# Second-level products placed differently in two PSUM tiles, and result stores issued from ScalarE's queue

## Chip, cores and metric

The kernel runs on one core of a Trainium2 chip. The metric is device time in microseconds (us) of one execution; the time before is the median of three runs. Engines are named as in the profile: PE is TensorE (PEld its weight loads), DVE is VectorE, ACT is ScalarE, POOL is GpSimd, SP is SyncE, which here only issues DMAs. A "q" behind an engine's name is its sequencer, which issues DMAs.

## What is computed

An attention block is followed by a feed-forward block. In the attention block (4 batches, 8 heads, 768 positions, 64 columns a head) queries and keys are assigned to 16 centroids, and a query attends only to keys of its own cluster. The result, 3072 x 512, is the input x of the second block, which the change concerns:

```python
def _moe_ref(x, w_in, w_out):
    h = x @ w_in            # (3072, 512) @ (512, 2048)
    r = np.maximum(h, 0.0)
    g = r * r
    return (g @ w_out).astype(np.float32)   # (3072, 2048) @ (2048, 512)
```

All is float32.

## The kernel before

The attention of all 16 pairs of heads comes first (to about 320 us), in an order written out by hand. Then the four batches go through the feed-forward block one after the other, in the order `FEED` = (1, 2, 3, 0). For each batch `up` makes g = relu(x w_in) squared, held transposed with the hidden dimension on the partitions, and a `down` function multiplies g by `w_out`.

Both products use a Strassen-like scheme: a matrix product is cut into 2 x 2 blocks, and seven block products of sums of blocks take the place of eight. The first batch uses `down` (L804), with one level of this scheme. It also prepares, in `make_right`, sums of the right-hand blocks for a second level and stores them in DRAM (`w_far`). During this first `down`, the hand-written order ends (`manual.close()`, L833); what comes after is put in order by the program that lays out the queues, by priorities and its own estimates, so the order on an engine can differ from that of the source.

The other three batches use `down_2` (L993). It treats 384 rows in two parts: a third of each half with one level (`product`, L1001, matmuls recorded at L1004) and two thirds with two levels (`second_level`, L903). `down_2` first issues three first-level products (1, 2, 4), then the whole second level, then calls `behind_pair`, which loads the next batch's x (`load_x`, L1108), then makes first-level products 7, 5, 6 and 3 and stores its own results (`osb`, L1039).

`second_level` goes through the seven outer products in the order `ORDER` = (5, 1, 7, 6, 2, 3, 4). Each is a group of seven inner products of 128 x 128 blocks with a contraction of 512, made by `times` (L894) as four float32 matmuls, which the trace records as eight matmuls and eight weight loads. In the text P1 to P7 are the seven in source order (L955 to L963). Within a group:

- `bank_tile` gives two PSUM tiles, `one` and `two`, each 128 x 512 float32, out of six such buffers. `spot(bank, i)` is the i-th block of 128 columns.
- P1 goes to block 0 of `one`, and ScalarE copies it out at once (`copied`, L956).
- P2, P3 and P5 go to `one` as well; P4, P6 and P7 go to `two`.
- P3, P4, P5 and P7 read their right operand from four slots (`slot(1)`, `slot(2)`, `slot(0)`, `slot(3)`) in SBUF. Each slot has one buffer; `load_right` (L879) issues the DMAs that refill them for the next group, four of 256 KB, on SP's queue.
- VectorE subtracts in place for P6's left operand (L958), between P2 and P6, prepares the left sums of the next group (`parts`, L930) and then adds the products up: four sums (L970 to L981) read PSUM, and `outer` (L914) adds their result r into c11, c12, c21, c22. After group 5, one more subtraction (L984) restores s2's sum for later groups.

At the end four DMAs of 256 KB (L986) store c22, c11, c12 and c21 in the output, on SP's queue. Of these tiles, c22 is complete after outer product 6, c11 after 2, c12 after 3 and c21 after 4.

When the next batch's x has come, `up` forms sums of it on VectorE (`x_sums`, L540, recorded at L538) and starts its matmuls (L767).

Of the kernel before, what the change touches and what calls it, by code (L numbers as in the profile page):

```python
# [18 lines left out]
P = 128  # L19
# [6 lines left out]
def kernel(  # L26
# [10 lines left out]
    nc = tc.nc  # L37
# [499 lines left out]
    def sub(out, a, b, eng=nc.vector):  # L537
        return eng.tensor_tensor(out=out, in0=a, in1=b, op=ALU.subtract)  # L538
# [161 lines left out]
    def bank_tile(width):  # L700
        return banks.tile([P, width], F32, name="bank", tag="bank")
# [142 lines left out]
    def right(j):  # L844
        return {1: w_q[0][0], 2: w_q[1][0], 3: w_q[1][1], 4: w_t[4], 5: w_t[1], 6: w_t[2],
                7: w_t[3]}[j]
# [11 lines left out]
    def s_home(i):  # L858
        return home[2 * i][:, 0 : F2 * PAIR].rearrange("p (f n) -> p f n", f=F2)

    def slot(k):
        first = F2 * PAIR + (k % 2) * F4 * P
        return home[k // 2 * 2][:, first : first + F4 * P].rearrange("p (f n) -> p f n", f=F4)

    def quarters(y):
        return [[y[:, F4 * g : F4 * (g + 1), P * m : P * (m + 1)] for m in range(2)] for g in range(2)]
# [12 lines left out]
    def load_right(j, *which):  # L879
        for k in which:  # L880
            nc.sync.dma_start(slot(k), w_far[j - 1, k].rearrange("p (f n) -> p f n", f=F4))

    def blocks(g, cols):
        return [[g[:, F2 * g2 : F2 * (g2 + 1), h, cols] for g2 in range(2)] for h in range(2)]
# [9 lines left out]
    def times(bank, left, rhs):  # L894
        for f in range(F4):
            nc.tensor.matmul(  # L896
                bank, lhsT=left[:, f], rhs=rhs[:, f], start=(f == 0), stop=(f == F4 - 1)
            )

    def plus(out, one, two):  # L900
        nc.vector.tensor_tensor(out=out, in0=one, in1=two, op=ALU.add)

    def second_level(b, g, sums_behind):  # L903
        a = blocks(g, slice(0, PAIR))
        s1, s2 = (s_home(i) for i in range(2))
        left = {1: a[0][0], 2: a[0][1], 3: s1, 4: a[1][1], 5: s1, 6: s2, 7: a[1][0]}
        work = xp.tile([P, KT * S], F32, name="work", tag="x1")
        c11, c12, c21 = (
            tp.tile([P, 4 * P], F32, name=f"c{to}", tag=f"x_t{t}")
            for to, t in ((11, 1), (12, 2), (21, 4))  # L910
        )
        c22 = spare.tile([P, 4 * P], F32, name="c22")

        def outer(j, r):  # L914
            if j == 1:
                plus(c12, c11, c22)
            elif j == 7:
                plus(c21, c11, r)
            elif j == 6:
                plus(c12, c12, r)  # L920
                plus(c21, c21, r)
                plus(c22, c22, c21)
            elif j == 2:
                plus(c11, c11, r)
            elif j == 3:
                plus(c12, c12, r)
            elif j == 4:
                sub(c21, c21, r)

        def parts(n):  # L930
            j = ORDER[n]
            x = [[left[j][:, F4 * g2 : F4 * (g2 + 1), P * i : P * (i + 1)] for g2 in range(2)]
                 for i in range(2)]
            s = sp.tile([P, 2, F4, P], F32, name="l2", tag=f"s{n % 2 + 1}")
            plus(s[:, 0], x[1][0], x[1][1])
            sub(s[:, 1], s[:, 0], x[0][0])
            sub(x[1][0], x[0][0], x[1][0])
            return x, s

        ahead = parts(0)  # L940
        yield
        for n, j in enumerate(ORDER):
            x, s = ahead
            y = quarters(right(j))
            first = 5 * P * (n % 2)
            copied = work[:, first : first + P]
            r = {5: c22, 1: c11}.get(j)
            if r is None:
                r = work[:, first + P : first + 5 * P]
            one, two = bank_tile(4 * P), bank_tile(4 * P)  # L950

            def spot(bank, i, n=1):
                return bank[:, P * i : P * (i + n)]

            times(spot(one, 0), x[0][0], y[0][0])  # L955
            nc.scalar.copy(out=copied, in_=spot(one, 0))  # L956
            times(spot(one, 1), x[0][1], y[1][0])
            sub(x[0][1], x[0][1], s[:, 1])  # L958
            times(spot(one, 2), s[:, 1], slot(1))
            times(spot(two, 0), x[1][0], slot(2))  # L960
            times(spot(one, 3), s[:, 0], slot(0))
            times(spot(two, 1), x[0][1], y[1][1])
            times(spot(two, 2), x[1][1], slot(3))  # L963
            if n + 1 < len(ORDER):
                ahead = parts(n + 1)
                load_right(ORDER[n + 1], 1, 2, 0, 3)
            else:
                sums_behind()

            plus(  # L970
                spot(r, 0, 2).rearrange("p (m n) -> p m n", m=2),
                spot(one, 1, 2).rearrange("p (m n) -> p m n", m=2),
                copied.unsqueeze(1).to_broadcast([P, 2, P]),
            )
            plus(spot(r, 2), spot(two, 0), spot(r, 1))
            plus(
                r.rearrange("p (i m n) -> p i m n", i=2, m=2)[:, :, 1],
                spot(one, 3).unsqueeze(1).to_broadcast([P, 2, P]),
                spot(r, 1, 2).rearrange("p (i n) -> p i n", i=2),
            )  # L980
            plus(spot(r, 1, 2), spot(two, 1, 2), spot(r, 1, 2))  # L981
            outer(j, r)
            if j == 5:
                sub(s1, a[0][1], s2)  # L984
        for to, (h, m) in ((c22, (1, 1)), (c11, (0, 0)), (c12, (0, 1)), (c21, (1, 0))):
            nc.sync.dma_start(  # L986
                out_view[b, NB * h : NB * h + 2, :, M2 * m : M2 * (m + 1)].rearrange(
                    "j p m -> p j m"
                ),
                to.rearrange("p (i m) -> p i m", i=2),  # L990
            )

    def down_2(b, g, behind_pair):  # L993
# [20 lines left out]
        def sums():  # L1014
# [3 lines left out]
            sub(a[1][0], a[0][0], a[1][0])  # L1018

        pair = second_level(b, g, sums)  # L1020
        next(pair)
        next(pair, None)
# [290 lines left out]
```

## Time and profile before

| | |
|---|---|
| time, median of 3 runs | 903.16 us (900.92 to 904.25) |
| time of the profiled execution | 900.14 us |
| span of the profiled execution, first to last instruction | 898.0 us |
| granted TensorE clock | 1.000 |
| second-level matmuls (L896) | x1176, first at 550.3, last at 878.4 us |
| copy of P1 (L956) | x21, 266 ns each |
| loads home<-w_far | x84, 256.0 KB each |
| stores out_dram<-c (L986) | x12, 256.0 KB each |

Lines of the profile name first the source line, the engine, the operation and its output and input, with buffer numbers left out: `bank` is a PSUM tile of `bank_tile`, `home` holds the slots and two of the left operands, `l` a pair of left sums, `g` the activations, `w_out` and `w_t` right operands, `work` the copy and r, `c` a result tile. In a timeline, a line begins with the start and the length of a run of like instructions in us. Weight loads overlap with matmuls. [...]

### The profile page before, as it was taken

The numbers are of one execution on the slowest core, as the hardware profiler recorded it, in microseconds if no ns is written. First come the engines' busy times: TensorE is split into PE (matmuls) and PEld (weight loads), VectorE is DVE, ScalarE is ACT, GpSimd is POOL, SyncE is SP. The second block draws the span as 40 slices with busy tenths as digits, with TensorE's granted clock in tenths as the row PEclk, the third lists the DMA queues.
The fourth block names the chain that finished last, engine by engine and source line by source line (L and its number), as shares of the span: only waits on it lengthen the run. The fifth ranks groups of instructions, "written<-read, shape, count | busy, mean of one in ns | idle before, by whom it ended". The sixth has DMA issues, their size and how long they took to land.

```text
span 898.0 us, 13177 instructions
## 1 busy us (share of the span) xinstructions
PE 889.4 (99%) x5043; PEld 583.8 (65%) x5043; DVE 680.9 (76%) x1107; ACT 321.3 (36%) x479; POOL 156.9 (17%) x168
## 2 busy tenths in 40 slices
PE   9999999999999999999999999999999999999997
PEld 5444444444444455578885559996557997556996
DVE  6798888888888999999525757757675785577683
ACT  5876677776676657630001110001111000111000
POOL 0000100000100257710022510013420004250000
PEclk9999999999999999999999999999999999999999
DMA  7767878677663246215400001560000563000351
GB/s 247 180 190 214 226 224 199 178 210 207 196 155 93 84 164 201 74 48 216 159 24 0 1 0 48 184 215 24 0 1 1 170 194 106 1 0 1 123 183 51
DMA packets 116442, 107.63 MB, mean 120 GB/s; under 512 B 56491, under 2 KB 93971, under 8 KB 115859
## 3 DMA queue, kind: packets, MB, share of 16 engines
q1 hardware_dynamic: 108130, 96.45, 36.0%
q10 hardware_dynamic: 8240, 10.26, 3.6%
q8 instruction: 42, 0.69, 0.3%
q14 instruction: 30, 0.24, 0.1%
HBM read 67.42 MB, written 28.25 MB: 107 GB/s over the span
## 4 chain that ended last, share of the span: by engine, by line
PE 91%; DVE 5%; DMA 1%; issue 1%; ACT 1%; DVEq 0%
PE bank L767 28%; PE bank L896 14%; PE sc L441 13%; PE av_a L475 9%; PE bank L821 8%; PE bank L1004 8%; PE av_b L475 4%; PE sc L450 3%; PE sc L329 1%; PE sc L494 1%; DVE g L724 1%; DVE w_raw L149 1%; DMA home<-w_far 1%; DVE w_raw L145 1%; DVE total L460 1%
## 5 line engine op out<-in xcount | busy, mean ns | idle before, releaser
L457 ACT ACTIVATE ex<-sc 128x1024 f32<-128x1024 f32 x144 | 144.4, 1026 | 38.0 <-PE sc L441 33.0
L724 DVE TENSOR_TENSOR g<-bank,g 128x384 f32<-128x384 f32 x192 | 102.6, 553 | 71.0 <-PE bank L767 67.9
L441 PE MATMUL sc<-qkT 64*128 64x512 f32 (+1 forms) x768 | 150.6, 484 | 0.0
L767 PE MATMUL bank<-xT,w_s 128*128 128x384 f32 x256 | 93.2, 487 | 0.9 <-DVE g L724 0.9
L767 PE MATMUL bank<-xT,w_in 128*128 128x384 f32 x256 | 93.2, 487 | 0.0
L441 PEld LDWEIGHTS sc<-qkT 64*128 64x128 f32 x768 | 65.9, 188 | 41.9 <-issue 30.1
L767 PE MATMUL bank<-x_t,w_s 128*128 128x384 f32 x256 | 93.0, 486 | 0.0
L475 PE MATMUL av_a<-ex,v_raw 128*64 128x512 f32 x384 | 85.9, 596 | 0.0
L558 POOL TENSOR_TENSOR w_s<-w_in 128x256 f32<-128x256 f32 x32 | 25.7, 804 | 337.4 <-PE bank L1004 155.7
L460 DVE TENSOR_TENSOR total<-total,ex 128x1024 f32<-128x1024 f32 x64 | 78.7, 1229 | 6.5
L161 POOL TENSOR_TENSOR w_in<-w_in,w_raw 128x512 int32<-128x512 int32 x16 | 22.1, 1379 | 295.2 <-DVE w_in L153 295.2
L730 ACT COPY g<-bank 128x384 f32<-128x384 f32 x32 | 15.3, 479 | 160.5 <-PE bank L767 160.5
L767 PEld LDWEIGHTS bank<-xT,w_s 128*128 128x128 f32 x256 | 48.5, 190 | 35.5 <-issue 2.1
L767 PEld LDWEIGHTS bank<-x_t,w_s 128*128 128x128 f32 x256 | 48.6, 190 | 33.9
L767 PEld LDWEIGHTS bank<-xT,w_in 128*128 128x128 f32 x256 | 48.5, 190 | 33.8 <-DVE g L538 0.6
L475 PEld LDWEIGHTS av_a<-ex,v_raw 128*64 128x64 f32 x384 | 26.1, 137 | 51.0 <-issue 50.7
L450 PE MATMUL sc<-rows 64*128 64x512 bf16 (+1 forms) x360 | 59.0, 323 | 0.3 <-DVE sums_t L503 0.3
L745 ACT ACTIVATE g<-g 128x384 f32<-128x384 f32 x53 | 27.4, 517 | 74.3 <-DVE g L724 74.3
L767 PE MATMUL bank<-x_t,w_in 128*128 128x384 f32 x128 | 46.5, 486 | 0.0
L956 ACT COPY work<-bank 128x128 f32<-128x128 f32 x21 | 5.6, 266 | 112.7 <-PE bank L896 112.7
L748 DVE SCALAR_TENSOR_TENSOR g<-g 128x384 f32<-128x384 f32 x75 | 43.5, 582 | 1.6
L896 PE MATMUL bank<-home,l 128*128 128x128 f32 x336 | 44.4, 275 | 0.0
(183 smaller groups left out, 1459.2 us busy)
## 6 DMA issues: line engine op xcount, KB each, us to landing
home<-w_far SPq DMA_DIRECT2D x84, 256.0 KB
words<-flat SPq DMA_DIRECT2D x26, 384.0 KB
w_raw<-in_moe_w_in_dram SPq DMA_DIRECT2D x16, 512.0 KB
w_raw<-in_moe_w_out_dram SPq DMA_DIRECT2D x16, 512.0 KB
w_far<-home SPq DMA_DIRECT2D x28, 256.0 KB
v_raw<-in_v_dram SPq DMA_DIRECT2D x16, 384.0 KB
rb<-far_r SPq DMA_DIRECT2D x32, 192.0 KB
q_raw<-in_q_dram ACTq DMA_DIRECT2D x12, 384.0 KB
```

The source lines that it names most:

```text
L441: nc.tensor.matmul(sc[i][:, e, cols], lhsT=qkT[pair][rows, NCH + c], rhs=qkT[pair][rows, n.start // P : n.stop // P], start=first, stop=no ...
L450: nc.tensor.matmul(sc[i][:, e, cols], lhsT=ohT[pair][rows, 1, c * P : (c + 1) * P], rhs=ohT[pair][rows, 0, columns(i)], start=first, stop= ...
L457: nc.scalar.activation(out=ex[i], in_=sc.pop(i), func=ACT.Exp, scale=SCALE)
L460: eng.tensor_tensor(out=out, in0=a, in1=b, op=ALU.add)
L475: nc.tensor.matmul(bank[D * e : D * (e + 1), 0 : n.stop - n.start], lhsT=raw_v[pair][:, e, c], rhs=ex[i][:, e, cols], start=c == 0, stop=c ...
L724: nc.vector.tensor_tensor(out=out, in0=bank, in1=to, op=ALU.add)
L745: nc.scalar.activation(out=to, in_=to, func=ACT.Relu)
L748: nc.vector.scalar_tensor_tensor(out=to, in0=to, scalar=0.0, in1=to, op0=ALU.max, op1=ALU.mult)
L767: nc.tensor.matmul(bank, lhsT=operands[j][0][:, kk], rhs=operands[j][1][:, kk], start=(kk == 0), stop=(kk == H2 - 1),)
L821: nc.tensor.matmul(bank, lhsT=left[:, f], rhs=right[:, f], start=(f == 0), stop=(f == F2 - 1))
L896: nc.tensor.matmul(bank, lhsT=left[:, f], rhs=rhs[:, f], start=(f == 0), stop=(f == F4 - 1))
L1004: nc.tensor.matmul(bank, lhsT=left[:, f], rhs=right(j)[:, f], start=(f == 0), stop=(f == F2 - 1))
```

## The change

The seven products keep their order in the source and their operands. P1 stays in block 0 of `one`. P2, P3, P4 and P5 go to blocks 0 to 3 of `two`, and P6 and P7 to blocks 1 and 2 of `one`. The four sums that read PSUM follow their products to the new places. The four stores of `second_level` are issued from ScalarE's queue instead of SP's.

```diff
             times(spot(one, 0), x[0][0], y[0][0])
             nc.scalar.copy(out=copied, in_=spot(one, 0))
-            times(spot(one, 1), x[0][1], y[1][0])
+            times(spot(two, 0), x[0][1], y[1][0])
             sub(x[0][1], x[0][1], s[:, 1])
-            times(spot(one, 2), s[:, 1], slot(1))
-            times(spot(two, 0), x[1][0], slot(2))
-            times(spot(one, 3), s[:, 0], slot(0))
-            times(spot(two, 1), x[0][1], y[1][1])
-            times(spot(two, 2), x[1][1], slot(3))
+            times(spot(two, 1), s[:, 1], slot(1))
+            times(spot(two, 2), x[1][0], slot(2))
+            times(spot(two, 3), s[:, 0], slot(0))
+            times(spot(one, 1), x[0][1], y[1][1])
+            times(spot(one, 2), x[1][1], slot(3))
...
             plus(
                 spot(r, 0, 2).rearrange("p (m n) -> p m n", m=2),
-                spot(one, 1, 2).rearrange("p (m n) -> p m n", m=2),
+                spot(two, 0, 2).rearrange("p (m n) -> p m n", m=2),
                 copied.unsqueeze(1).to_broadcast([P, 2, P]),
             )
-            plus(spot(r, 2), spot(two, 0), spot(r, 1))
+            plus(spot(r, 2), spot(two, 2), spot(r, 1))
             plus(
                 r.rearrange("p (i m n) -> p i m n", i=2, m=2)[:, :, 1],
-                spot(one, 3).unsqueeze(1).to_broadcast([P, 2, P]),
+                spot(two, 3).unsqueeze(1).to_broadcast([P, 2, P]),
                 spot(r, 1, 2).rearrange("p (i n) -> p i n", i=2),
             )
-            plus(spot(r, 1, 2), spot(two, 1, 2), spot(r, 1, 2))
+            plus(spot(r, 1, 2), spot(one, 1, 2), spot(r, 1, 2))
             outer(j, r)
...
         for to, (h, m) in ((c22, (1, 1)), (c11, (0, 0)), (c12, (0, 1)), (c21, (1, 0))):
-            nc.sync.dma_start(
+            nc.scalar.dma_start(
                 out_view[b, NB * h : NB * h + 2, :, M2 * m : M2 * (m + 1)].rearrange(
```

## The prediction

> **What bounds the kernel now.** I read the page's table of engines first, then the chain that ended last, then the timeline of one second-level group, then the waits.
>
> ```profile
> PE 889.4 (99%) x5043; PEld 583.8 (65%) x5043; DVE 680.9 (76%) x1107; ACT 321.3 (36%) x479; POOL 156.9 (17%) x168
> PE 91%; DVE 5%; DMA 1%; issue 1%; ACT 1%; DVEq 0%
> ```
>
> TensorE is occupied 99% of the span and is 91% of the chain, so only time taken out of TensorE's own stream shortens the kernel. The change touches one stage, the second-level products (L955 to L963, all recorded at L896), which run three times, for the batches after the first. The view of three stretches, each from the first second-level matmul to the start of the next L1004 product, gives their length:
>
> ```profile
> 550.31:595.52 45.21, 45.05 (x394) 44.29 (x392) 33.21 (x58) 2.24 (x8) 0.00 (x0) 1.00 0.54 163
> 691.93:737.15 45.22, 45.05 (x393) 44.34 (x392) 33.28 (x58) 2.23 (x8) 0.00 (x0) 1.00 0.53 164
> 833.57:878.56 44.99, 44.99 (x394) 44.37 (x392) 33.22 (x58) 2.24 (x8) 0.00 (x0) 1.00 0.50 159
> ```
>
> Columns: length, then busy time of TensorE, its weight loads, VectorE, ScalarE and GpSimd, clock, DMA share and GB/s. TensorE looks full (45.05 of 45.21), but a matmul's end is modelled, so the busy sum hides short gaps; starts must be compared. The timeline of one group (seven products P1 to P7 in source order, eight instructions each) shows them:
>
> ```profile
> 563.16 1.06 PE L896 MATMUL bank<-w_t,g 128*128 128x128 f32 x8
> ...
> 564.05 0.61 PE L896 MATMUL bank<-home,g 128*128 128x128 f32 x4
> 564.25 0.27 ACT L956 COPY work<-bank 128x128 f32<-128x128 f32 x1 [6.16 <-PE bank L896]
> 564.57 0.97 PEld L896 LDWEIGHTS bank<-w_t,g 128*128 128x128 f32 x8
> 564.57 1.16 PE L896 MATMUL bank<-w_t,g 128*128 128x128 f32 x8
> ...
> 565.57 1.06 PE L896 MATMUL bank<-home,l 128*128 128x128 f32 x8
> ...
> 566.46 0.61 PE L896 MATMUL bank<-home,g 128*128 128x128 f32 x4
> ...
> 566.91 1.06 PE L896 MATMUL bank<-home,l 128*128 128x128 f32 x8
> ...
> 567.80 1.06 PE L896 MATMUL bank<-w_t,g 128*128 128x128 f32 x8
> ...
> 568.70 1.06 PE L896 MATMUL bank<-home,g 128*128 128x128 f32 x8
> ```
>
> P1 starts at 563.16; half of P4 (x4) at 564.05; P2 at 564.57; P3 at 565.57; the rest of P4 at 566.46; P5, P6, P7 follow. P2 writes the PSUM tile `one`, which ScalarE is reading (L956), so P2 waits for the copy; whatever planned the order has put half of P4, which goes to `two`, into the hole. The copy ends at 564.25 + 0.27 = 564.52 and P2's first weight load starts at 564.57. Elsewhere a load starts about 0.11 us ahead of its matmul; here both stand at 564.57.
>
> The waits, the chain of the first stretch and its timeline show two further small stops (this one and its like at 712.44), both at that early half of P4, whose right operand comes by DMA:
>
> ```profile
> PE bank L896 <- DMA home<-w_far: 0.3, 2, 0.2
> ```
>
> ```profile
> 586.38 3.57 DMA home<-w_far
> ```
>
> ```profile
> 590.09 0.68 PE L896 MATMUL bank<-home,g 128*128 128x128 f32 x4 [0.16 <-DMA home<-w_far]
> ```
>
> The slot that P4 reads is refilled only after the other half of P4 of the group before; from there to its next use is 3.5 us, as long as the load (3.57).
>
> **What the Trainium skill says.** "PSUM — Partial Sum Buffer", section on bank collisions, says that two engines must be kept off one PSUM bank at the same time, so writer and reader of a tile are put in sequence even where their columns differ. The trace agrees: P2 starts 0.05 us after the copy's end. "TensorE: Matmul & The Clock Gate", Part 2, says that weight loads are pulled ahead of running matmuls while matmuls keep their order. The trace agrees (0.11 us lead), and shows the lead lost where the product had to wait. The same page, architectural detail, has ScalarE and VectorE as strict FIFO, which is what makes a store on ScalarE's queue a risk; no view of before shows a store there. "DMA: Bandwidth & Descriptors", on issuing engines, says that queues of different engines share the same 16 DMA engines; so the move brings no bandwidth.
>
> **The change part by part.** First, the tiles. After it P1 goes to `one`, P2 to P5 to `two`, P6 and P7 to `one`. P2 no longer follows the copy's read; P6 does, but starts five products after P1.
>
> The pitch of one product without a wait is (568.70 - 566.91) / 2 = 0.895; over four products, 837.32 to 840.89, it is 3.57 / 4 = 0.8925 us. A batch has 7 x 7 = 49 products, 43.73 us. The three stretches exceed this by 1.48, 1.49 and 1.26: 4.23 us in all. An ordinary group gives 563.16 to 569.59 = 6.43, against 7 x 0.8925 = 6.25: 0.18 lost, of it 0.07 from the end of half P4 to P2 (0.52 instead of 0.446 us) and 0.11 of weight load in the open (P2 to P3 takes 1.00 instead of 0.89). 21 x 0.18 = 3.8; the two stops on the DMA bring the other 0.4. That the 0.11 belongs to the wait is seen at 590.61: where the DMA made P4 late and the copy was already over, P2's load is ahead again and P2 to P3 takes 0.89.
>
> What comes next, once the hole is gone? P3 needs sums made a group ahead by VectorE; the trace has them done several us early (l<-g at 568.41, used after 576). P6 needs x[0][1] minus a sum (L958), possible 0.2 us after P2, that is 1.98 us after P1; P6 starts at 5 x 0.8925 = 4.46, which leaves 2.5 us for an operation of 0.69. Its queue is VectorE's: in the worst order, the three sums that become readable after P5 (pitch 0.35, 0.24, 0.36), the next three preparations (2.05), P7's sum (0.36) and the outer sums (three at most, 1.97, once a batch; else one, 0.69) stand before it: 5.33 us from P5's end, which is 1.58 before the next P1. It would then end 5.33 - 1.58 + 0.69 = 4.44 after P1, just before 4.46, and elsewhere at 3.2. After a batch's first group L984 (2.28) stands in place of outer sums: 4.75, 0.3 us late, 0.9 in all. VectorE has 33.2 us of work in each stretch of 43.7, 76%. P4 as a whole moves behind P3, so every slot has from its last use to its next six products, 5.35 us, against loads of 3.57: both DMA stops go. I charge nothing for these covers; if VectorE's fails, P6 stalls for what is missing.
>
> The copy L956 is still 0.27 and now has 3.5 us of cover. The sums L970 to L981 read the same columns with the same shapes, so the same durations; two of them can start before P7 instead of after it. That takes about 0.8 us of VectorE work from between P7 and the end, which only helps.
>
> Second, the stores. Twelve DMAs of 256 KB leave SP's queue for ScalarE's. On SP each takes 0.39 us of issue and waits for its sum (21.0 us of waits at L986 in all, mostly at the batch's end where nothing is behind). ScalarE is busy 2.2 us of 45 in the stage, so 12 x 0.4 is free there. A store that waits on ScalarE holds back the copy behind it: c22 is ready 4.48 us after a P1 (576.02 to 580.50), c12 4.13 after (588.87 to 593.00). If these two were queued ahead of that group's copy, P6 would start at about 4.48 + 0.39 + 0.27 + 0.05 = 5.2 instead of 4.46: 0.7 lost, and 0.4 for c12, 3.3 us over three batches. If queued where they become ready, nothing. I take nothing and keep 3.3 for the range. On SP the loads that stood behind a store issue up to 0.4 us earlier; the xT load at 599.13 does too, but TensorE does not wait for it now (up starts at 609.34 without a gap), so no gain. In flight, store and slot loads now share; 256 KB at the 362 GB/s seen at 601 to 603 is 0.7 us (estimate), and 3.57 + 0.7 stays below 5.35.
>
> Sum: -4.2 us; bounds from 0 (3.3 given back by the stores and 0.9 by VectorE) to -4.2, since that is the whole excess over the pitch. Against the profiled execution: 900.14 - 4.2 = 895.9. The median of the runs shown is 903.16, 3.0 above that execution; the same subtraction gives 899.0.
>
> **Rivals.** A, forecast: the hole goes, 899.0. For it: the copy's end and P2's start fit to 0.05 us; against it: the planner had already filled most of the hole, so only 0.18 per group is there to take.
>
> B: it does only part of what it says. The order after L833 is not written by hand; a plan over other estimates may again cut a product in two or set stores ahead of copies. With 3.3 us given back the sum is -0.9, 902.3. For it: the trace shows such a rearrangement now; against: with no product behind a fresh read there is nothing to rearrange for.
>
> C: more comes out, because the replanned boundaries also tighten, for instance in the 5.0 us from the last VectorE sum's end (892.57 + 0.42) to 898.0. There is no TensorE gap there to gain from, so I allow 2 us beyond A: 896.9.
>
> D, slower: at the batch boundary VectorE stands idle waiting for the x load (L538 on xT, 6.96 and 7.62 us). If the plan sets that waiting subtraction before the sum s2 (L1025, 1.22 us) that product 6 needs at about 602.5, s2 ends at 605.62 + 0.96 + 1.22 = 607.8 and TensorE stalls 5.3 us, at two boundaries 10.6. Net +6.4, 909.6. It decides from the moment s2 is queued behind the wait. For it: the wait stands in VectorE's FIFO today; against: s2 was done by 595.6, ten us before, and comes earlier in the source.
>
> **Numbers.** A 0.62, B 0.14, C 0.08, D 0.16. Half a per cent of the median, 4.5 us, is about what a measurement of this kernel can tell from no change; A sits just inside it. The runs shown spread by 3.3 us, so A's own range is 897 to 901, with 0.28 of its 0.62 beyond the bound; with C, faster has 0.36. Same has 0.34 of A and 0.14 of B: 0.48. Slower has 0.16. The range runs from 896 to 905; it leaves out most of D and a small part of A and C.
>
> **What would show it.** Right: products in source order at a pitch of 0.89 with no half products, P2's weight load 0.1 ahead of its matmul, groups of 6.25 us, stretches near 43.8, no wait of TensorE on home<-w_far. Wrong on tiles: a group still above 6.4, or P6 starting late behind VectorE or the copy. Wrong on stores: ScalarE's copy late behind a store. Slower: a gap in TensorE between the L1004 products and L767.

## The result, and the profile after

The kernel after takes 895.83 us (median of 6 runs, 895.62 to 897.37), the kernel before 901.52 us (6 runs, 900.68 to 904.25). The ratio is 0.9934, 95% interval 0.9919 to 0.995: by the ratio 5.9 us faster, between 4.5 and 7.3; the two medians lie 5.7 apart. The forecast was 899.0, range 896.0 to 905.0: right in direction and place, too small in size, and the median lies 0.17 us below the range. Taken from profile to profile, the prediction had 895.9, and the profiled execution took 895.67.

The profiled execution of the kernel after has a span of 893.9 us, 4.1 less than that of before. In the view of stretches, cut at the same instructions as before (first second-level matmul to the next first-level product; same columns), the three are now alike:

```profile
550.21:593.98 43.77, 43.77 (x394) 43.77 (x392) 31.69 (x59) 2.24 (x8) 0.00 (x0) 1.00 0.58 173
690.40:734.17 43.77, 43.77 (x394) 43.77 (x393) 31.70 (x59) 2.24 (x8) 0.00 (x0) 1.00 0.59 174
830.58:874.35 43.77, 43.77 (x393) 43.77 (x392) 31.69 (x59) 2.24 (x8) 0.00 (x0) 1.00 0.54 163
sum 131.31, PE 131.31 PEld 131.31 DVE 95.09 ACT 6.71 POOL 0.00; mean PE 43.77 PEld 43.77 DVE 31.70 ACT 2.24 POOL 0.00
```

The sum was 135.42. It fell by 4.11, so in this pair of profiles the whole difference of the spans (4.1) lies in the stage that was changed. Between the stretches nothing changed: from the end of one to the start of the next it is 96.4 us in both profiles. The figure for the weight loads tells it best: weight loads now cover every instant of the stretch (43.77 of 43.77, before 44.29 of 45.21), because no product starts with its load in the open.

The timeline of the same group as before (the third of the first stretch) shows the products in source order, P1 and P2 merged into one run of 16:

```profile
562.71 1.95 PE L896 MATMUL bank<-w_t,g 128*128 128x128 f32 x16
...
563.81 0.27 ACT L956 COPY work<-bank 128x128 f32<-128x128 f32 x1 [5.99 <-PE bank L896]
...
564.50 1.06 PE L896 MATMUL bank<-home,l 128*128 128x128 f32 x8
564.93 0.68 DVE L538 TENSOR_TENSOR g<-g,l 128x512 f32<-128x512 f32 x1
...
565.39 1.06 PE L896 MATMUL bank<-home,g 128*128 128x128 f32 x8
...
566.29 1.06 PE L896 MATMUL bank<-home,l 128*128 128x128 f32 x8
...
567.18 1.06 PE L896 MATMUL bank<-w_t,g 128*128 128x128 f32 x8
```

A run of eight is 1.06 us long and the next one starts 0.89 later, so the lengths overlap and starts are compared. The copy ends at 564.08 and the next write of its tile is P6 at 567.18. P6's left operand is ready at 564.93 + 0.68 = 565.61, 1.6 us ahead. The next group starts at 568.97, 6.26 after this one. In the list of waits no line is left in which TensorE waits for home<-w_far, the loads of the slots.

ScalarE's own timeline shows the four stores of one batch between the copies. The first number in brackets is ScalarE's idle time before a copy; it is 6.04 instead of 5.99 behind the first store, and 5.99 again behind the second, so no copy is held back by more than 0.05 us:

```profile
576.31 0.27 ACT L956 COPY work<-bank 128x128 f32<-128x128 f32 x1 [5.99 <-PE bank L896]
579.36 0.39 ACTq L986 DMA_DIRECT2D out_dram<-c  x1
582.62 0.27 ACT L956 COPY work<-bank 128x128 f32<-128x128 f32 x1 [6.04 <-PE bank L896]
583.80 0.39 ACTq L986 DMA_DIRECT2D out_dram<-c  x1
588.87 0.27 ACT L956 COPY work<-bank 128x128 f32<-128x128 f32 x1 [5.99 <-PE bank L896]
591.20 6.21 ACTq L986 DMA_DIRECT2D out_dram<-c  x2
```

Two questions remained. Does the gain come from the wait, from the places in PSUM as such, or from the stores? And why is it 5.7 us between the medians when the two profiles differ by 900.14 - 895.67 = 4.5?

### The profile page after: what moved, and what is told of

It is laid out like the page before. It is cut to its first block, busy times and chain, and to the rows that moved or that the text cites. A ratio compares the mean times of both kernels' runs of the same rounds, so it can differ in the third digit from the quotient of the medians.

```text
span 893.9 us, 13219 instructions
## 1 busy us (share of the span) xinstructions
PE 885.3 (99%) x5043; PEld 581.7 (65%) x5043; DVE 676.4 (76%) x1107; ACT 321.3 (36%) x479; POOL 157.1 (18%) x168
## 4 chain that ended last, share of the span: by engine, by line
PE 92%; DVE 4%; DMA 2%; issue 1%; ACT 1%; ACTq 0%; DVEq 0%; SPq 0%
PE bank L767 30%; PE bank L896 15%; PE sc L441 12%; PE av_a L475 8%; PE bank L821 8%; PE bank L1004 8%; PE av_b L475 4%; PE sc L450 3%; PE sc L329 1%; PE sc L494 1%; DMA qkT<-words 1%; DVE g L724 1%; DVE total L460 1%; DVE w_raw L149 1%; DVE w_raw L145 1%
## 5 line engine op out<-in xcount | busy, mean ns | idle before, releaser
L767 PE MATMUL bank<-xT,w_s 128*128 128x384 f32 x256 | 93.2, 487 | 0.8 <-DVE g L724 0.8
L767 PE MATMUL bank<-xT,w_in 128*128 128x384 f32 x256 | 93.2, 487 | 0.0
L767 PE MATMUL bank<-x_t,w_s 128*128 128x384 f32 x256 | 93.0, 486 | 0.0
L767 PEld LDWEIGHTS bank<-xT,w_s 128*128 128x128 f32 x256 | 48.5, 190 | 35.4 <-issue 2.0
L767 PEld LDWEIGHTS bank<-x_t,w_s 128*128 128x128 f32 x256 | 48.6, 190 | 33.9
L767 PEld LDWEIGHTS bank<-xT,w_in 128*128 128x128 f32 x256 | 48.5, 190 | 33.8 <-DVE g L538 0.6
L767 PE MATMUL bank<-x_t,w_in 128*128 128x384 f32 x128 | 46.5, 486 | 0.0
```

Of the source, the lines that this page charges most:

```text
L767: nc.tensor.matmul(bank, lhsT=operands[j][0][:, kk], rhs=operands[j][1][:, kk], start=(kk == 0), stop=(kk == H2 - 1),)
```

## The experiments

Theory W, named in the expectations: TensorE loses 0.18 us at each of 21 writes behind a fresh read, and, apart from that, stops on the load of P4's slot, whose window (3.4 to 3.5 us) is as short as the load is long. The rivals: R, spread of the runs; S, the stores; T, writing the two tiles in turn pays as such; M, something outside the stretches.

**e1: the kernel before, unchanged.**

> The kernel before, unchanged, as a null test. Theory W (the wait behind the copy, 21 times 0.18 us, and a load that is on the edge): ratio 1.000, three second-level stretches of 45.0 each plus 0.2 to 0.3 for every stop on a home<-w_far load; the number of these stops differs from one execution to the next, so this execution need not have two. Theory R (the rest of the gain, 5.7 measured less 4.1 in the spans, is spread of the runs of before): the executions lie between 900 and 904, with nothing in the second-level stretches that differs. Both: the profile outside the stretches is as in the first one within 0.5 us.

Ratio 0.9999 (0.999 to 1.0009), 14 runs from 899.8 to 904.24. Its chain of waits has one stop in the second stretch, and the stretches are 44.98, 45.36 and 45.05:

```profile
692.35 16.61 PE bank L896 x144
708.98 3.71 DMA home<-w_far
712.83 24.88 PE bank L896 x216
```

(Columns: start, length, what the chain ran through.) A stretch with holes alone is 44.98 long, and that repeats to a hundredth; the stops do not repeat: two of 0.2 in the first profile, here one of 0.4 (and 0.06 more in the third stretch, where the list of waits names no load). The null ratio leaves nothing to rival R but the choice of the base.

**e2: the tiles alone.** The kernel after with its stores back on SP:

```diff
-            nc.scalar.dma_start(
+            nc.sync.dma_start(
                 out_view[b, NB * h : NB * h + 2, :, M2 * m : M2 * (m + 1)].rearrange(
```

> The tiles are changed, the stores stay on SP. Theory W: the stretches are 43.8 each, no TensorE wait on home<-w_far, span near 893.9, ratio as that of the whole change (0.9934). Rival S (moving the stores off SP's queue brings the part of the gain that the prediction did not have, 1 to 1.5 us): ratio near 0.995, and slot loads late behind a store.

Ratio 0.9943 (0.993 to 0.9956), median 895.69, stretches 43.77 three times, span 893.9, no wait on home<-w_far. This is one stretch in the chain of waits:

```profile
550.22 43.77 PE bank L896 x392
```

The median is that of the kernel after (895.83) to 0.14 us: within the interval, the tiles bring all of it.

**e3: the stores alone.** The same line changed the other way in the kernel before.

> The stores move to ScalarE, the tiles stay. Theory W: the half product and the hole stay in every group, stretches 45.0 to 45.2, ratio 0.999 to 1.001. Rival S: 1 to 1.5 us faster, ratio 0.9985, with the stops on home<-w_far gone.

Ratio 1.0001 (0.9991 to 1.001). TensorE's order is that of before. The stops were not gone, and one was worse:

```profile
710.69 1.06 PE L896 MATMUL bank<-w_t,home 128*128 128x128 f32 x8
713.01 0.68 PE L896 MATMUL bank<-home 128*128 128x128 f32 x4 [1.26 <-DMA home<-w_far]
```

```profile
708.21 4.67 DMA home<-w_far
```

P1 starts at 710.69, the early half of P4 at 713.01 instead of 711.58, 1.4 us late. The chain gives 4.67 us for the load that it waited for (the single line above), against 3.58 at the same place in the first profile. The store of c22 is not issued before a later group (722.96), so it isn't the cause. The stretches are 45.16, 46.42 and 45.21, 136.79 in all. The stores do cost something here, but little: in five of the six groups that follow a store, the copy comes about 0.05 us later and P2 starts 0.58 us behind the half of P4 instead of 0.52, 0.3 us in all, which is inside the interval (in the sixth a stop hides it). Rival S falls.

**e4: only the order of the source.** Tiles and stores of before, P4 moved between P1 and P2:

```diff
             nc.scalar.copy(out=copied, in_=spot(one, 0))
+            times(spot(two, 0), x[1][0], slot(2))
             times(spot(one, 1), x[0][1], y[1][0])
             sub(x[0][1], x[0][1], s[:, 1])
             times(spot(one, 2), s[:, 1], slot(1))
-            times(spot(two, 0), x[1][0], slot(2))
```

> The tiles and stores of before; only the source order is P1, P4, P2, P3, P5, P6, P7, so that all of P4, which writes the other tile, stands between P1 and P2. Theory W (it is the wait, not the place in PSUM, that costs): no weight load in the open at P2, groups of 6.25, and stretches of 43.8 plus the stops on the slot of P4, which is still read second in its group: its load goes out behind that of P3's slot, 3.6 us before its next use, as long as the load takes. So 43.8 to 45, at least 3 us faster in all. Rival T (alternating tiles as such is what pays): the stretches stay at 45.0.

Ratio 0.9951 (0.9938 to 0.9963). The chain has 43.77 in each stretch, as with the new tiles:

```profile
551.82 43.77 PE bank L896 x392
...
692.00 43.77 PE bank L896 x392
...
832.19 43.77 PE bank L896 x392
```

Rival T falls: P2 and P3 still go to the tile that was read, and a whole product in between covers the copy. The expectation was wrong on the stops: there were none. On SP's queue the load of P4's slot goes out first here (572.39, with P1 at 570.41 and P4's next use at 577.56), not behind that of P3's slot, so its window is 5.2 us. This profile's second level starts 1.45 us later than that of after (551.82 against 550.37 in the chain), in code that is the same; the span, 895.3, is longer by that. It is spread of the part before: the kernel after itself begins at 551.22 in e6.

**e5: one product put back behind the read.** The kernel after with P2 in `one` again; P3, P4, P5 in `two`, P6 and P7 in `one`:

```diff
-            times(spot(two, 0), x[0][1], y[1][0])
+            times(spot(one, 1), x[0][1], y[1][0])
...
+            plus(spot(r, 0), spot(one, 1), copied)
+            plus(spot(r, 1), spot(two, 0), copied)
```

> The kernel after with one product put back behind the fresh read: P2 in `one`, P3 to P5 in `two`, P6 and P7 in `one`; the sum of P2 and P3 becomes two sums. Half of P3 fills the hole instead of half of P4. Theory W: each group 6.43 again with P2's weight load in the open, stretches 45.0; P3's slot has about 4.5 us from its last use to its next, so no TensorE wait on home<-w_far, and the time is 3.7 us above the kernel after. If stops on P4's slot are what the kernel before loses beyond the 4.2 us, this kernel is also 0.3 to 1.3 us faster than before (ratio 0.9985 to 0.9997); if they are rare, ratio 1.000. Theory T (both tiles written in turn is what pays, not the wait): stretches 43.8.

Stretches of 45.23 each, no stop, median 900.9, against 896.29 for the kernel after in the same comparison. The hole is back, filled by half of P3 (first line):

```profile
565.94 0.61 PE L896 MATMUL bank<-home,l 128*128 128x128 f32 x4
566.50 1.16 PE L896 MATMUL bank<-w_t,g 128*128 128x128 f32 x8
```

It costs 0.21 us a group instead of 0.18: in most groups P2 starts 0.56 behind that half instead of 0.52, since the copy itself starts 0.05 us later behind P1; why was not tried. Against before the ratio is 0.999 (0.998 to 1.0001), although its stretches sum to 135.69, more than the 135.42 of the first profile of before. About 0.35 us of the difference lies outside the span (see "What stays open" below). The rest fits stops that are larger on the average than in the first profile, but the interval holds 1, so it isn't shown here.

**e6: the kernel after, unchanged.**

> The kernel after, unchanged, for the size of the effect. Theory W: stretches 43.77 each, ratio 0.9943 to 0.9955 (4.1 in the stretches, 0.35 outside the span, and 0 to 0.7 of varying stops on P4's slot that only the kernel before has). Theory M (more than the stretches): ratio 0.9930 to 0.9940 again.

Ratio 0.9934 again (0.9915 to 0.9954), stretches of 43.77 again. The value lies where theory M put it; the interval holds what W expected as well. The excess over W's figures is not in this kernel, whose stretches repeat to a hundredth. Nor do the profiles show it elsewhere in the span: between the stretches every profile of this document has 96.41 or 96.42 us, and 19.3 to 19.7 behind the last one; only the start of the first stretch varies, from 549.7 to 552.2, in kernels of both kinds. What is left is the stops of the kernel before, which e9 to e11 look at.

**e7: eight copies instead of one, in the kernel after.**

```diff
-            nc.scalar.copy(out=copied, in_=spot(one, 0))
+            for _ in range(8):
+                nc.scalar.copy(out=copied, in_=spot(one, 0))
```

> The kernel after with the copy of P1 made eight times instead of once, 1.9 us more work on ScalarE between P1 and the first later write of `one`. Theory W: P6 starts 3.4 us after P1's end and the eight copies need 8 x 0.27 = 2.2, so nothing is lost: stretches 43.8 to 43.9, the time of the kernel after. If the length of the read itself costs TensorE, 1.9 x 21 = 40 us slower.

Median 895.91, stretches 43.77, 43.77 and 43.86. The copies take 2.35 us in a row and end at 565.69, P6 starts at 566.71:

```profile
563.34 2.35 ACT L957 COPY work<-bank 128x128 f32<-128x128 f32 x8 [3.90 <-PE bank L896]
```

So the cover over the copy is real, and seven more reads of one tile while the other is written cost 0.09 us in all.

**e8: two copies in the kernel before.** The same edit with `range(2)`.

> The kernel before with the copy of P1 made twice, which makes the hole 0.27 us longer; three of P4's four matmuls (0.67 us) stand in it instead of two. Theory W: P2 waits for the second copy's end, 0.05 us after it; a group takes 6.25 + 0.14 (hole left) + 0.11 (weight load in the open) = 6.50, stretches 45.5 plus stops on home<-w_far. If the matmuls put into the hole hid all of the wait but the weight load, 6.36 and 44.5.

The hole grew as worked out, to 45.50 in the two stretches without a stop: three of P4's four matmuls stand in it, and the weight load of P2 is still in the open; the second has a stop of 1.5 us behind a load of 4.74:

```profile
551.56 45.50 PE bank L896 x392
...
693.48 16.83 PE bank L896 x144
710.52 4.74 DMA home<-w_far
715.39 25.10 PE bank L896 x216
...
836.90 45.50 PE bank L896 x392
```

Median 903.08, ratio 1.0005 (0.9987 to 1.0022); the 1.5 us of larger holes are within the interval.

**e9: the load of P4's slot in two halves.** The kernel before, holes kept, the stops' cause taken away:

```diff
         for k in which:
-            nc.sync.dma_start(slot(k), w_far[j - 1, k].rearrange("p (f n) -> p f n", f=F4))
+            src = w_far[j - 1, k].rearrange("p (f n) -> p f n", f=F4)
+            for f in (slice(0, 2), slice(2, 4)) if k == 2 else (slice(0, 4),):
+                nc.sync.dma_start(slot(k)[:, f], src[:, f])
```

> The kernel before; only the load of P4's slot is made in two halves of 128 KB, one for each half of P4, so that the half that is used early is also refilled early and has 5.4 us until its next use instead of 3.4. The holes stay. Theory W with stops as a second part: three stretches of 44.99, no TensorE wait on home<-w_far, 0.4 to 1.5 us faster than before (ratio 0.9983 to 0.9996), 4.0 slower than the kernel after. If the stops count for nothing outside the profiles: ratio 1.000.

Ratio 0.9982 (0.9973 to 0.9991): 1.6 us faster than before, between 0.8 and 2.4. Its stretches hold the holes and nothing else, 134.95 us in all, and TensorE waits for no load of a slot:

```profile
550.01:594.99 44.98, 44.98 (x393) 44.28 (x392) 33.20 (x58) 2.23 (x8) 0.00 (x0) 1.00 0.58 166
691.41:736.39 44.98, 44.98 (x393) 44.29 (x392) 33.21 (x58) 2.23 (x8) 0.00 (x0) 1.00 0.55 167
832.81:877.79 44.98, 44.98 (x393) 44.29 (x392) 33.21 (x58) 2.23 (x8) 0.00 (x0) 1.00 0.56 159
```

**e10 and e11: two more profiles of the kernel before.**

> The kernel before, one more profile, to see how the stops on P4's slot vary: stretches of 44.99 plus 0.2 to 1.5 in those that have a stop; a sum over the three of 135.4 to 136.8.

> As the run before it: a sum of the three stretches of 135.4 to 136.8, with the stops at places that need not be the same.

Sums of 136.40 and 135.45. In e10 the waits and the chain of the second stretch read:

```profile
PE bank L896 <- DMA home<-w_far: 1.1, 2, 0.7
```

```profile
708.82 4.12 DMA home<-w_far
729.58 3.05 DMA home<-w_far
```

The five profiles whose TensorE order is that of before:

| profile | three stretches, us | sum | above 134.95 (e9) |
|---|---|---|---|
| first, before | 45.21, 45.22, 44.99 | 135.42 | 0.47 |
| e1 | 44.98, 45.36, 45.05 | 135.39 | 0.44 |
| e3 | 45.16, 46.42, 45.21 | 136.79 | 1.84 |
| e10 | 44.99, 46.17, 45.24 | 136.40 | 1.45 |
| e11 | 44.98, 45.19, 45.28 | 135.45 | 0.50 |

The mean of the last column is 0.94, and 0.72 without e3, whose stores differ from those of before. Nearly all of it is stops on P4's slot; not so are the 0.3 us of larger holes in e3 and, in e10, a P5 about 0.1 us late. The first profile was one of the small ones.

## Why the prediction was right and wrong

**Where the kernel is bound, and what the wait is.** Right. e2 gives the whole effect with the tiles alone, e4 gets the same stretches by order alone, and e5 brings the hole back by putting one product behind the read.

**The size of the holes.** Right. They were put at 0.18 a group, 3.8 in all. e9, which has only the holes, measures 134.95 - 131.31 = 3.64; the pitch, put at 0.8925, is 43.77 / 49 = 0.8933.

**The 0.11 us of weight load in the open.** It was included in the 0.18, and the after profile has it gone: weight loads cover the stretch. e8's two clean stretches of 45.50, worked out with it, agree with it.

**The two stops on P4's slot.** The mechanism was right, and this is the step that failed: the term of the sum was mis-sized. The prediction gave them "the other 0.4" and set the bound at -4.2 "since that is the whole excess over the pitch". That was the excess in one execution. A load whose window is as long as its usual time ends late by an amount that varies: five profiles have 0.4 to 1.8 above the holes, mean 0.9, and taking the cause away (e9) is worth 1.6 by the clock (0.8 to 2.4). Holes and stops then make 3.6 + 0.9 to 3.6 + 1.6, instead of 4.2.

**The base.** A second number failed beside it. The forecast subtracted from 903.16, the median of three runs with a spread of 3.3. More runs of the same kernel put it at 901.3 to 901.9, which is 1.3 to 1.8 lower. With 901.5 and the same -4.2 the forecast would have been 897.3. The base and the stops erred to the same side, and the lower end of the range, 896, had no room for both. For the same reason "same" was given more chance than "faster": 4.2 lies inside half a per cent, 5.9 outside.

**Covers costed at nothing.** P6's operand is 1.6 us ahead where the worst order left nothing, since the order in fact sets the subtraction early. L984's feared 0.3 us doesn't appear: the stretches are 43.77 = 49 products. The copy's cover was tested by e7. These costs came out at nothing, as charged.

**The stores.** Costed at 0, and e3 gives 1.0001; the 0.05 us by which a store sets back the next copy vanish under the cover of the new tiles. Rival B's place, a store ahead of a copy, did not come up: all copies in the ScalarE timeline come before the stores that would have held them.

**D, the slower rival.** Its place exists in the profile after too (VectorE waits for the x load 14.2 us in two times), but s2 stands before that wait as it did, and the L767 matmuls follow the L1004 products without a gap. **C** put 2 us more at the replanned boundaries and the kernel's end; from the end of the last stretch to the end of the span it is 19.45 us before and 19.54 after, so nothing came from there.

**What stays open.** The time outside the span (execution less span) is 1.77 to 1.90 us in the profiles of after, e2, e4, e5, e6 and e7, and 2.09 to 2.18 in those of before, e1, e3, e8, e9, e10 and e11, the kernels that put part of P4 early. It is so in the unprofiled executions too, whose spans are on record: 1.73 to 1.93 against 2.09 to 2.27, the medians about 0.35 apart. These 0.35 us are part of the gain, a term that the prediction did not have, and no run tells what they are. Holes, the mean of the profiles and this make 3.64 + 0.94 + 0.35 = 4.9, with e9's value for the stops 5.6; the interval of the result, 4.5 to 7.3, holds both. The recorded spans speak for the second: in the comparison of e6 their medians are 899.7 and 894.45, 5.25 apart, and 3.64 and 1.6 make 5.24. No trace of an unprofiled execution shows the stops themselves. Nothing in the runs points to a version beyond the kernel after in this stage, whose TensorE stream has no gap left.

## What to carry to other kernels

Where a matmul writes a PSUM tile that another engine has just begun to read, put a whole product into another tile between them, by place or by order (here 0.89 us of work over a copy of 0.27); half a product hid most of the wait but not the weight load behind it. A wait that one profile shows with 0.2 us, on a transfer whose window equals its length, should be costed from several profiles: give it a range up to the longest load seen, and take the base time from more than three runs before setting the end of a range. A busy share of 99% on TensorE hid 3% of a stage; the starts of like products, and the share of the weight loads, showed it.

## What had not been expected

The same 256 KB load, issued at the same place of the program (near 708.5 us in the second stretch of before), took 3.58, 3.71, 4.12 and 4.67 us in four executions (the first profile, e1, e10 and e3), and 4.74 in e8, two us later. Why its length varies so was not tried. In e11 the chain does not name it, though the half of P4 starts about 0.1 us late at that place (712.17).
